# First batch of a spectral-mixing and SwiGLU kernel: tables and filter loaded whole, weights rounded through the first chunk, filter parts on partition halves

## The chip, the cores and the metric

The kernel runs on one core of one Trainium2 chip. The metric is the device time of one execution in microseconds (us). Every time quoted is the median of several executions with its lowest and highest.

## The reference, cut to what matters

```python
X = np.fft.rfft(x, axis=1)                 # x: (8, 3008, 256) float32
y = np.fft.irfft(X * (filt_r + 1j * filt_i)[None], n=3008, axis=1)
y = y.astype(np.float32).reshape(24064, 256)
g = y @ w_gate                              # 256 x 1536, float64
out = ((g / (1 + np.exp(-g))) * (y @ w_val)) @ w_out   # 1536 x 256, float64
```

The three weight matrices arrive as float64 and are brought to fp32 on the chip.

## The kernel before

The Fourier transforms are matmuls in three stages. Stage 1 (`pa`) is a 47-point transform of x, written to DRAM as d1. Stage 2 reads d1 back as `t2`, transforms it over 64 points (`pb`), multiplies it with the filter on VectorE (`p`, `q`), adds on GpSimd, transforms back (`pc`), and writes d2. Stage 3 (`pd`) reads d2 and gives y. The feed-forward follows in blocks of 14 products (`wA_g` and the like; a seven-product scheme for 2x2 blocks of matrices); after every three blocks comes a projection (`wA_o`, `wE_o`, ...), 64 projections in all. The kernel places the tiles that its matmuls write in PSUM; copying one out of it is called its eviction (0.59 us for `g` from a pc of 128x512, on ScalarE). Between the stages results wait in tiles: `t1` (stage 1, on the way to d1), `g` (pc, on the way to d2) and `y`; `s` and `h` hold the two branches of the feed-forward, whose gating product VectorE makes, and `w` and `pw` are the working tiles of a rounding. While batch b goes through the feed-forward, pieces of batch b+1's transforms are filled in between the products. Only batch 0 has nothing to hide under: its transforms, and the rounding of the weights, are the start of the run.

Stage 2, its loads, and one rounding (18 such parts in all):

```python
def load_two(self, u):                       # tables, t2 and filter of one step
    self.tb[u] = tbpool.tile([128, NV, 2, 128], FP32, tag="tb")           # 2 buffers
    nc.sync.dma_start(out=self.tb[u], in_=de_dram[:, ss])
    self.t2[u] = t2pool.tile([128, NV, C], FP32, tag="t2")                # 3 buffers
    self.f[u] = fpool.tile([128, NV, 2, C], FP32, tag="f")
    for p in range(2):
        half = slice(64 * p, 64 * p + 64)
        nc.sync.dma_start(out=self.t2[u][half], in_=self.d1[...])
        nc.sync.dma_start(out=self.f[u][half], in_=f_dram[:, ss])

def stage2a(self, u):
    ps = fps.tile([128, NV, C], FP32, name=f"pb_{self.b}_{u}", tag="f")   # PSUM, 2 buffers
    # ... two matmuls into ps ...
    nc.vector.tensor_tensor(out=pt, in0=ps, in1=f[:, :, 0, :], op=ALU.mult)
    nc.vector.scalar_tensor_tensor(out=qt[lo], in0=ps[hi], scalar=-1.0, in1=f[hi, :, 1, :], ...)
    nc.vector.tensor_tensor(out=qt[hi], in0=ps[lo], in1=f[lo, :, 1, :], op=ALU.mult)
    add(nc.gpsimd, pt, pt, qt)

def stage2b(self, u):
    ps = fps.tile([128, NV, C], FP32, name=f"pc_{self.b}_{u}", tag="f")   # the same two buffers
    # ... two matmuls into ps ...
    nc.scalar.copy(out=g, in_=ps)
    # ... two stores of g to d2, issued by GpSimd ...

def round_weights(j):
    # ... nine VectorE operations on 128 x 512 elements: exponent, sign, mantissa, product ...
    # then three ScalarE copies and four GpSimd adds into wg_t, wv_t or wo_t
```

The order of the start, with cuts:

```python
for k, filt in enumerate((filt_r, filt_i)):  # rearranged copy of the filter in DRAM
    ...nc.scalar.dma_start(out=f_dram[...], in_=...)
for u in range(N_ONE):                       # 16 steps
    spec.stage1(u)
for u in range(N_TWO + 1):                   # 12 steps
    spec.stage2a(u); spec.stage2b(u - 1)
    round_weights(todo.pop(0))
# ... stage 3 of the first chunk ...
while todo:
    round_weights(todo.pop(0))
```

Of the kernel before, what the change touches and what calls it, by code (L numbers as in the profile page):

```python
# [44 lines left out]
NJ = NM // 2  # L45
# [56 lines left out]
def kernel(  # L102
# [22 lines left out]
    t1pool = pool("t1", 2)  # L125
    t2pool = pool("t2", 3)
    fpool = pool("fp", 2)
# [16 lines left out]

    f_dram = fdpool.tile([NQ, NS, 2, C], FP32, name="filt")

# [8 lines left out]
    def weight_parts():  # L155

        cols = [w.bitcast(U32).rearrange("(a p) (h j f two) -> j p h a f two",
                                         a=2, p=128, h=2, j=NJ, two=2)
                for w in (moe_w_gate, moe_w_val)]
        rows = moe_w_out.bitcast(U32).rearrange("(l j p) (c f two) -> j p l c f two",  # L160
                                                l=2, j=NJ, p=128, c=2, two=2)
        for j in range(NJ):
            for w, dst in zip(cols, (wg_t, wv_t)):
                yield w[j], dst[:, j], True
            yield rows[j], wo_t[:, j], False

# [3 lines left out]
    def load_weights(j):  # L170
        if j < len(weights):
            raws[j] = rpool.tile([128, 2, 2, 128, 2], U32, name=f"raw_{j}", tag="raw")
            for i in range(2):
                nc.sync.dma_start(out=raws[j][:, i], in_=weights[j][0][:, i])

    def round_weights(j):



        load_weights(j + 1)  # L180
        raw, (_, dst, left) = raws.pop(j), weights[j]
# [3 lines left out]
        man = w.bitcast(U32)  # L185
        v = nc.vector
        v.tensor_scalar(out=pw, in0=high, scalar1=20, scalar2=0x7FF,
                        op0=ALU.logical_shift_right, op1=ALU.bitwise_and)
        v.tensor_scalar(out=pw, in0=pw, scalar1=-896.0, scalar2=0.0, op0=ALU.add, op1=ALU.max)
        v.tensor_scalar(out=pw, in0=pw, scalar1=255.0, scalar2=None, op0=ALU.min)  # L190
        v.tensor_scalar(out=pw, in0=pw, scalar1=23, scalar2=None, op0=ALU.logical_shift_left)
        flat = "p a b f -> p (a b f)"
        flat2 = "p a b f two -> p (a b f) two"
        v.scalar_tensor_tensor(out=pw.rearrange(flat), in0=raw.rearrange(flat2)[:, :, 1],
                               scalar=0x80000000, in1=pw.rearrange(flat),
                               op0=ALU.bitwise_and, op1=ALU.bitwise_or)
        v.tensor_scalar(out=man, in0=high, scalar1=0xFFFFF, scalar2=None, op0=ALU.bitwise_and)
        v.tensor_scalar(out=w, in0=man, scalar1=2.0 ** -20, scalar2=1.0,
                        op0=ALU.mult, op1=ALU.add)
        v.scalar_tensor_tensor(out=w.rearrange(flat), in0=raw.rearrange(flat2)[:, :, 0],  # L200
                               scalar=2.0 ** -52, in1=w.rearrange(flat),
                               op0=ALU.mult, op1=ALU.add)
        v.tensor_tensor(out=w, in0=w, in1=pw.bitcast(FP32), op=ALU.mult)
        e = nc.gpsimd
# [17 lines left out]
    class Spectral:  # L222
# [10 lines left out]
        def load_x(self, u):  # L233
            if u < N_ONE:
                self.x[u] = xpool.tile([NR, NV, C], FP32, name=f"x_{self.b}_{u}", tag="x")
                rows = x[self.b].rearrange("(r n) c -> r n c", n=32)

                for r in (slice(0, 80), slice(80, NR)):
                    nc.sync.dma_start(out=self.x[u][r], in_=rows[r, ts(u, NV), :])

        def load_two(self, u):
            if u < N_TWO:
                b = self.b
                ss = ts(u, NV)
                self.tb[u] = tbpool.tile([128, NV, 2, 128], FP32, name=f"tb_{b}_{u}", tag="tb")
                nc.sync.dma_start(out=self.tb[u], in_=de_dram[:, ss])
                self.t2[u] = t2pool.tile([128, NV, C], FP32, name=f"t2_{b}_{u}", tag="t2")
                self.f[u] = fpool.tile([128, NV, 2, C], FP32, name=f"f_{b}_{u}", tag="f")
                for p in range(2):
                    half = slice(64 * p, 64 * p + 64)  # L250
                    a0 = p * NS + NV * u
                    nc.sync.dma_start(out=self.t2[u][half],
                                      in_=self.d1[a0:a0 + NV].rearrange("s n c -> n s c"))
                    nc.sync.dma_start(out=self.f[u][half], in_=f_dram[:, ss])

# [4 lines left out]
        def stage1(self, u):  # L260

            if u == 0:
                self.load_x(0)
                self.load_x(1)
            self.load_x(u + 2)
            t1 = t1pool.tile([NK, NV, C], FP32, name=f"t1_{self.b}_{u}", tag="t1")
            ps = fps.tile([128, NV, C], FP32, name=f"pa_{self.b}_{u}", tag="f")
            nc.tensor.matmul(out=ps[0:NK], lhsT=wf_t, rhs=self.x.pop(u), start=True, stop=True)  # L268
            nc.scalar.copy(out=t1, in_=ps[0:NK])
            nc.gpsimd.dma_start(out=self.d1_rows[:, ts(u, NV), :], in_=t1)  # L270

        def stage2a(self, u):
# [6 lines left out]
            for i in range(NV):  # L279
# [4 lines left out]
            lo, hi = slice(0, 64), slice(64, 128)  # L284
            nc.vector.tensor_tensor(out=pt, in0=ps, in1=f[:, :, 0, :], op=ALU.mult)
            nc.vector.scalar_tensor_tensor(out=qt[lo], in0=ps[hi], scalar=-1.0,
                                           in1=f[hi, :, 1, :], op0=ALU.mult, op1=ALU.mult)
            nc.vector.tensor_tensor(out=qt[hi], in0=ps[lo], in1=f[lo, :, 1, :], op=ALU.mult)
            add(nc.gpsimd, pt, pt, qt)
# [167 lines left out]


    nc.sync.dma_start(out=wf_t, in_=wf_dram.ap())
    for k, filt in enumerate((filt_r, filt_i)):  # L460
        for half in range(2):
            off, step = (0, 1) if half == 0 else (N1, -1)
            nc.scalar.dma_start(
                out=f_dram[32 * half:32 * half + 32, :, k, :],
                in_=bass.AP(tensor=filt.tensor, offset=filt.offset + off * C,
                            ap=[[N1 * C, 32], [step * C, NS], [1, C]]))
    nc.scalar.dma_start(out=wi_t, in_=wi_dram.ap())
    spec = Spectral(0)
    with tc.tile_pool(name="raw", bufs=2) as rpool:
        for u in range(N_ONE):  # L470
            spec.stage1(u)
        load_weights(0)
        todo = list(range(len(weights)))
        for u in range(N_TWO + 1):
            if u < N_TWO:
                spec.stage2a(u)
            if u:
                spec.stage2b(u - 1)
            round_weights(todo.pop(0))
        for i in range(2):  # L480
            spec.load_t4(0, i)
        for step in range(4):
            spec.stage3(0, step)
        while todo:
            round_weights(todo.pop(0))

    spool = pool("sp", 2)
    hpool = pool("hp", JB + 1)
    upool = pool("up", 2)
    opool = pool("op", 2)  # L490

# [4 lines left out]
    for b in range(B):  # L496
# [26 lines left out]
        for i in range(NP):  # L523
# [5 lines left out]
            def fill(fills=fills):  # L529
                for piece in fills.pop(0):  # L530
                    piece()

            hidden(b, k, j, cur.y[k], fill)
            if late is not None:
# [35 lines left out]
```

## Time and profile before

The kernel before took 3158.5 us (3158.22 to 3161.21, 3 runs). The table gives landmarks of its profiled execution, read from the timeline of TensorE. A stage's length is the difference of two columns. (The fifth is counted from the second product, `wE_o`, of the second projection to that of the last.)

| first pb | last pc starts | first feed-forward product | first projection | second to 64th projection | span |
|---|---|---|---|---|---|
| 65.42 | 148.09 | 167.98 | 224.57 | 2858.63 | 3156.1 |

The fifth column is the body: there TensorE is busy all the time (2893.15 of 2900 us from 220 to 3120 us), so a microsecond gained before the first projection should be a microsecond off the end. The columns before it are the start, where TensorE waits. The prediction shows the profile's own lines.

### The profile page before, as it was taken

To read this page: it belongs to the slowest core of one execution; us is meant where nothing else is said; L and a number is where in the kernel's file an instruction comes from. 1 tells how busy PE (TensorE), PEld (TensorE's weight loads), DVE (VectorE), ACT (ScalarE), POOL (GpSimd) and SP (SyncE) were. 2 spreads that over 40 slices of the span, in tenths; PEclk is the share of its full clock that TensorE was granted. 3 is DMA by queue.
4 is the path that set the end of the run, shared out by engine and by line. 5 is a ranking of instruction groups with operands and counts; after the bars stand their busy time and mean duration, and the time that the engine had idled before them with its cause. 6 is when DMAs were issued, how large, how long until landed. Compare 5 with 4: busy or idle time off the path is not lost.

```text
span 3156.1 us, 40788 instructions
## 1 busy us (share of the span) xinstructions
PE 3047.2 (97%) x15488; PEld 2243.0 (71%) x15488; DVE 1432.8 (45%) x2306; ACT 1144.6 (36%) x2104; POOL 1387.8 (44%) x1644
## 2 busy tenths in 40 slices
PE   4499999999999999999999999999999999999998
PEld 1266777777776777777777677777777677777776
DVE  4654454345444445335443345434544444544443
ACT  1144334333334333333334433333333433333332
POOL 3444454345443445344444445434544345533343
PEclk9689999999999999999999999999999999999999
DMA  7732332224222233123322233222331223210000
GB/s 224 206 96 70 97 81 73 60 60 111 81 59 70 72 89 96 55 63 88 87 73 60 70 91 87 66 67 60 104 87 55 71 66 93 71 30 20 21 9 12
DMA packets 118291, 240.78 MB, mean 76 GB/s; under 512 B 21712, under 2 KB 55504, under 8 KB 118096
## 3 DMA queue, kind: packets, MB, share of 16 engines
q1 hardware_dynamic: 88224, 160.00, 18.3%
q0 software_dynamic: 26624, 75.01, 8.2%
q10 hardware_dynamic: 3248, 3.18, 0.3%
q8 instruction: 122, 2.00, 0.3%
q14 instruction: 73, 0.60, 0.1%
HBM read 163.13 MB, written 78.12 MB: 76 GB/s over the span
## 4 chain that ended last, share of the span: by engine, by line
PE 83%; POOL 7%; DVE 3%; issue 3%; ACT 1%; DMA 1%; SPq 0%; POOLq 0%; DVEq 0%; ACTq 0%
PE wA_g L357 15%; PE wA_v L357 15%; PE wA_o L421 8%; PE wE_g L357 7%; PE wE_v L357 7%; PE wE_o L421 7%; PE wF_o L421 4%; PE wF_g L357 4%; PE wF_v L357 4%; PE pd L315 4%; POOL o L148 3%; PE pa L268 3%; POOL h L151 3%; PE pb L280 3%; PE pc L297 3%
## 5 line engine op out<-in xcount | busy, mean ns | idle before, releaser
L357 PE MATMUL wA_g<-y,wg_t 128*128 128x376 f32 x1536 | 612.6, 480 | 1.0 <-ACT s L377 1.0
L357 PE MATMUL wA_v<-y,wv_t 128*128 128x376 f32 x1536 | 611.0, 479 | 0.0
L151 POOL TENSOR_TENSOR h<-h 128x376 f32<-128x376 f32 x576 | 564.9, 981 | 28.8
L148 POOL TENSOR_TENSOR h<-h 128x376 f32<-128x376 f32 x192 | 187.7, 978 | 732.1 <-PE wE_v L357 388.7
L366 ACT COPY u_g<-wA_g 128x376 f32<-128x376 f32 x576 | 269.5, 468 | 627.3 <-PE wA_g L357 627.3
L357 PEld LDWEIGHTS wA_v<-y,wv_t 128*128 128x128 f32 x1536 | 291.7, 190 | 194.4 <-DVE h L379 11.7
L421 PEld LDWEIGHTS wA_o<-wo_t,h 128*128 128x128 f32 x3456 | 406.3, 192 | 16.3
L421 PE MATMUL wA_o<-wo_t,h 128*128 128x128 f32 x3456 | 417.5, 275 | 0.0
L357 PEld LDWEIGHTS wA_g<-y,wg_t 128*128 128x128 f32 x1536 | 283.0, 190 | 176.7 <-issue 27.4
L148 DVE TENSOR_TENSOR s<-u_g,wF_g 128x376 f32<-128x376 f32 x192 | 104.9, 546 | 516.0 <-PE wF_g L357 492.4
L384 ACT ACTIVATE s<-s 128x1128 f32<-128x1128 f32 x192 | 219.5, 1143 | 320.8 <-DVE s L148 320.8
L386 DVE TENSOR_TENSOR h<-s,h 128x1128 f32<-128x1128 f32 x192 | 256.0, 1333 | 125.3 <-ACT s L384 125.2
L357 PE MATMUL wE_g<-y,wg_t 128*128 128x376 f32 x768 | 306.0, 480 | 0.0
L357 PE MATMUL wE_v<-y,wv_t 128*128 128x376 f32 x768 | 305.9, 480 | 0.0
L366 ACT COPY u_v<-wA_v 128x376 f32<-128x376 f32 x576 | 272.3, 473 | 72.0 <-PE wA_v L357 68.3
L421 PE MATMUL wE_o<-wo_t,h 128*128 128x128 f32 x2304 | 281.6, 276 | 7.5 <-DVE o L148 7.5
L421 PE MATMUL wF_o<-wo_t,h 128*128 128x128 f32 x2304 | 278.4, 275 | 0.0
L421 PEld LDWEIGHTS wE_o<-wo_t,h 128*128 128x128 f32 x2304 | 267.5, 192 | 13.6 <-DVE o L148 13.6
L421 PEld LDWEIGHTS wF_o<-wo_t,h 128*128 128x128 f32 x2304 | 267.7, 192 | 0.0
L148 DVE TENSOR_TENSOR s<-u_g,wE_g 128x376 f32<-128x376 f32 x384 | 209.1, 544 | 103.8 <-ACT u_g L366 99.8
L148 DVE TENSOR_TENSOR h<-u_v,wE_v 128x376 f32<-128x376 f32 x384 | 209.2, 545 | 28.4 <-ACT u_v L366 5.6
L357 PEld LDWEIGHTS wE_g<-y,wg_t 128*128 128x128 f32 x768 | 146.5, 191 | 97.4 <-issue 0.9
(67 smaller groups left out, 3180.4 us busy)
## 6 DMA issues: line engine op xcount, KB each, us to landing
f<-filt SPq DMA_DIRECT2D x192, 256.0 KB
tb<-de_tbl SPq DMA_DIRECT2D x96, 256.0 KB
d<-t POOLq DMA_DIRECT2D x128, 192.0 KB, 2.4
t<-d SPq DMA_DIRECT2D x192, 128.0 KB
d<-g POOLq DMA_DIRECT2D x192, 128.0 KB, 2.7
t<-d SPq DMA_DIRECT2D x64, 384.0 KB
x<-in_x_dram SPq DMA_DIRECT2D x128, 160.0 KB
out_dram<-o POOLq DMA_DIRECT2D x128, 128.0 KB, 2.0
```

Of the source, the lines that this page charges most:

```text
L148: eng.tensor_tensor(out=dst, in0=a, in1=b, op=ALU.add)
L151: eng.tensor_tensor(out=dst, in0=a, in1=b, op=ALU.subtract)
L268: nc.tensor.matmul(out=ps[0:NK], lhsT=wf_t, rhs=self.x.pop(u), start=True, stop=True)
L280: nc.tensor.matmul(out=ps[:, i, :], lhsT=self.tb[u][:, i, 0, :], rhs=t2[:, i, :], start=True, stop=True)
L297: nc.tensor.matmul(out=ps[:, i, :], lhsT=tb[:, i, 1, :], rhs=pt[:, i, :], start=True, stop=True)
L315: nc.tensor.matmul(out=psv[:, n, :], lhsT=self.t4[k, i][:, n, ts(cb, 128)], rhs=wi_t, start=True, stop=True)
L357: nc.tensor.matmul(out=bk[z][kind], lhsT=wt[z][:, j, LEFT[p], :], rhs=y[:, RIGHT[p], :], start=start, stop=True, skip_group_check=True)
L366: nc.scalar.copy(out=u[(1, 6, 7).index(p)], in_=bk[z]["A"])
L384: nc.scalar.activation(out=s[:, 0:3], in_=s[:, 0:3], func=AF.Silu)
L386: nc.vector.tensor_tensor(out=h[:, 0:3], in0=s[:, 0:3], in1=h[:, 0:3], op=ALU.mult)
L421: nc.tensor.matmul(out=bk[kind][:, t, :], lhsT=hs[i][:, HID[p], t0:t0 + 128], rhs=wo_t[:, JB * q + i, RIGHT[p], :], start=start and t == 0 ...
```

## The change

Its intent: give batch 0 the memory that the feed-forward uses only later, and load the stage-2 tables and the whole filter into it at once, so that no load is left in the stage-2 loop; load x in four pieces; take VectorE's work for the weights from nine operations to six and spread the second half of it over the first chunk's blocks. The filter's real and imaginary parts lie on partitions 0 to 63 and 64 to 127, which halves its loads and its tile, at the price of four half-size products in place of three. The diff, cut:

```diff
-    t2pool = pool("t2", 3)
+    t2pool = pool("t2", 2)
-    f_dram = fdpool.tile([NQ, NS, 2, C], FP32, name="filt")
+    f_dram = fdpool.tile([128, NS, C], FP32, name="filt")
     # ... rounding: order of the parts; load_weights(j + 2) ...
+        v.tensor_scalar(out=man, in0=high, scalar1=0xFFFFF, scalar2=None, op0=ALU.bitwise_and)
+        nc.scalar.activation(out=w, in_=man, func=AF.Copy, scale=2.0 ** -20, bias=1.0)
         v.tensor_scalar(out=pw, in0=high, ...)
         v.tensor_scalar(out=pw, in0=pw, scalar1=-896.0, scalar2=0.0, op0=ALU.add, op1=ALU.max)
-        v.tensor_scalar(out=pw, in0=pw, scalar1=255.0, scalar2=None, op0=ALU.min)
-        v.tensor_scalar(out=pw, in0=pw, scalar1=23, scalar2=None, op0=ALU.logical_shift_left)
+        v.tensor_scalar(out=pw, in0=pw, scalar1=255.0, scalar2=2.0 ** 23, op0=ALU.min, op1=ALU.mult)
-        v.tensor_tensor(out=w, in0=w, in1=pw.bitcast(FP32), op=ALU.mult)
+        nc.gpsimd.tensor_tensor(out=w, in0=w, in1=pw.bitcast(FP32), op=ALU.mult)
     # ... load_x: for batch 0, four loads of 8 positions ...
+        def load_tables(self, parts=3):
+            tb = spool0.tile([128, NS, 2, 128], FP32, name="tb0")
+            f = spool0.tile([128, NS, C], FP32, name="f0")
+            for i in range(parts):
+                nc.sync.dma_start(out=tb[:, ts(i, n)], in_=de_dram[:, ts(i, n)])
+                for rows, view in filter_parts():        # four pieces of 32 partitions
+                    nc.sync.dma_start(out=f[rows, ts(i, n), :], in_=view(n * i, n))
     # ... stage1: four t1 buffers for batch 0 ...
-            nc.vector.tensor_tensor(out=pt, in0=ps, in1=f[:, :, 0, :], op=ALU.mult)
+            for h in (lo, hi):
+                nc.vector.tensor_tensor(out=pt[h], in0=ps[h], in1=fr, op=ALU.mult)
     # ... start: with a pool "start" that ends before the feed-forward's pools begin ...
+        spec.load_x(0); load_weights(0); load_weights(1); spec.load_tables()
-    opool = pool("op", 2)
+    opool = pool("op", 1)
     # ... first chunk:
+            if b == 0 and i == 0:
+                for rows, view in filter_parts():
+                    nc.scalar.dma_start(out=f_dram[rows], in_=view(0, NS))
+            for _ in range((2, 3, 2, 2, 2, 3)[i] if todo else 0):
+                round_weights(todo.pop(0))
```

## The prediction

> **What bounds the kernel now.** I read the busy slices of the page first. Over the body TensorE is busy in nine tenths of every slice; only the first two slices (79 us each) stand at four.
>
> ```profile
> PE   4499999999999999999999999999999999999998
> DVE  4654454345444445335443345434544444544443
> PEclk9689999999999999999999999999999999999999
> ```
>
> So I split the run into windows. From 220 to 3120 us TensorE is busy 2893 of 2900 us: nothing is to be won there, and what the change does to the other engines there (VectorE 45%) costs nothing unless it becomes a wait. The start is another matter. Columns: stretch, length, then busy us (instructions) of PE, weight loads, DVE, ACT, POOL, granted clock, DMA share, GB/s.
>
> ```profile
> 20.00:40.00 20.00, 11.32 (x13) 2.85 (x13) 10.77 (x22) 5.60 (x19) 9.75 (x19) 1.00 0.73 220
> 80.00:100.00 20.00, 10.84 (x24) 7.34 (x24) 6.20 (x9) 1.68 (x4) 7.22 (x9) 0.74 0.69 197
> 140.00:160.00 20.00, 5.83 (x12) 3.67 (x12) 18.02 (x33) 3.26 (x11) 10.59 (x18) 0.50 0.75 218
> 180.00:200.00 20.00, 15.38 (x38) 8.36 (x37) 12.96 (x23) 9.12 (x18) 7.58 (x15) 0.66 0.40 123
> 200.00:220.00 20.00, 20.00 (x64) 11.71 (x64) 10.03 (x16) 9.44 (x18) 9.53 (x11) 1.00 0.00 0
> ```
>
> TensorE is busy 206.75 us of the first 300, so about 93 us of idle is all that can be gained, and part of the busy time is at a low clock. In that start four stretches follow each other, read from the timeline: stage 1 of batch 0 (to 54 us), stage 2 (65.4 to 150.2), the round trip of stage 3 through DRAM (150.2 to 168.0, the first feed-forward product), and a disturbed first feed-forward block (168 to about 200).
>
> Stage 1 and stage 2 wait for buffers. From the lists of waits up to 205 us, the sync queue's own and then ScalarE's (total us, times, longest):
>
> ```profile
> SPq L246 <- PE pc L297: 39.3, 11, 7.1
> SPq L239 <- PE pa L268: 26.2, 16, 6.2
> ...
> ACT t L269 <- DMA d<-t: 30.9, 15, 6.7
> ```
>
> L246 is the load of a table pair, which may go only when the second transform (pc) two steps back has freed one of two buffers. One step of stage 2 on the timeline:
>
> ```profile
> 88.90 2.04 PE L280 MATMUL pb<-t,tb 128*128 128x256 f32 x4 [3.43 <-issue]
> 90.98 0.69 DVE L285 TENSOR_TENSOR p<-pb,f 128x512 f32<-128x512 f32 x1 [5.08 <-DMA t<-d]
> 91.68 0.69 DVE L286 SCALAR_TENSOR_TENSOR q<-pb,f 64x512 f32<-64x512 f32 x1
> 92.39 0.68 DVE L288 TENSOR_TENSOR q<-pb,f 64x512 f32<-64x512 f32 x1
> 92.58 0.33 SPq L246 DMA_DIRECT2D tb<-de_tbl  x1
> 94.13 1.27 POOL L148 TENSOR_TENSOR p<-p,q 128x512 f32<-128x512 f32 x1
> 95.80 2.04 PE L280 MATMUL pb<-t,tb 128*128 128x256 f32 x4 [3.25 <-DMA tb<-de_tbl]
> ```
>
> The reader is to see 6.9 us from pb to pb: 3.7 from pb's start until the table load is issued, 3.2 until the table is there. VectorE's products were over at 93.1, so without that load pb could have gone 2.7 us earlier.
>
> The disturbed block: VectorE still had some four weight roundings queued ahead of the first evictions.
>
> ```profile
> 187.00 0.69 DVE L203 TENSOR_TENSOR w<-w,pw 128x512 f32<-128x512 f32 x1
> 190.03 0.55 DVE L148 TENSOR_TENSOR s<-u_g,wF_g 128x376 f32<-128x376 f32 x1 [2.34 <-POOL wo_t L151]
> ```
>
> Between 168.0 and 200.3 TensorE did 19 feed-forward products, 7 pa and two steps of pd: 19 x 0.63 + 7 x 0.86 + 2 x 0.45 = 18.9 us at full clock (durations from 330 to 347 us and the chain), so 13.4 us were lost.
>
> [...] from 10 to 22 us ScalarE's queue took 53.1% and the sync queue 48.9% of the engines' time. [...] The trace has 689 ns on 128 and 684 on 64 partitions, so a half costs as much as a whole. [...] the masking of a weight took 0.42 us alone, 1.49 beside a GpSimd add. [...] Here pb takes 2.04 us at a stretch's mean clock of 0.74, and some 0.86 in the body.
>
> **The change part by part**, with the order of instructions as the changed program builds it.
>
> (1) Stage 1. x comes in four loads instead of sixteen, with four t1 buffers instead of two: the 26 us and 31 us of waits above mostly go. But the sync queue now holds tables and filter ahead of t2. Until the first t2 load: x 3.1, tables 3.1, filter 3.1, four weight parts 1.0 MB; besides them d1 3.1 MB written, and the DRAM copy of the filter, 3.1 MB, which the scheduler puts first on ScalarE's queue although the source issues it in the first feed-forward block. Sum 16.6 MB (before: 15.8 MB in 70 us). The best stretch, 10 to 22 us, moved 344 GB/s, the mean was 225. At 320 that is 52 us; with 3 us for t2, pb starts at 55 instead of 65.4. Gain 10, uncertain by 6.
>
> (2) Stage 2. The table load leaves the loop; p is now two products on halves, four at 0.69 = 2.8 us. The loop that is left goes through the one PSUM buffer that pb reuses: 2.0 (pb) + 2.8 + 0.2 for hand-overs = 5.0 us. Where TensorE gets the full clock pb takes 1 us and the loop 4. I take 4.7 on average. Some 14 rounding operations of about 0.55 us lie in between, mostly under pb. First two steps 2.1 + 5.6, ten more 47, last add and pc 3.4: 58 us, plus 2 for stalls: 60 instead of 84.8. Gain 25, uncertain by 7.
>
> (3) Stage 3 stays: 17.8 us from the last pc to the first product. So the feed-forward begins at 55 + 60 + 18 = 133 instead of 168: 35 us.
>
> (4) Rounding. Nine operations on VectorE become six; the linear step goes to ScalarE (0.58 us), the last product to GpSimd (about 1.3). By the means of the groups before (0.75, 0.42, 0.47, 0.56, 0.72, 0.74) six cost 3.7 us. But in the built order only nine of 18 are done before y; the others sit among the evictions of blocks 0 to 3, with single buffers for w and pw. VectorE there: 8.7 roundings x 3.7 = 32, plus four blocks' evictions at 6 x 0.545 + 0.55 + 1.33 = 5.15 each, 20.6, together 52.6 us; plus about 1 us per rounding for GpSimd's product and four adds before w may be overwritten: 61. TensorE needs 4 x 14 x 0.63 + 8 x 0.86 + 0.9 = 43. VectorE becomes the bound of these blocks: 18 us lost instead of 13.4. Cost 5, range -3 to +12.
>
> (5) Body. The extra half product is 84 x 0.69 = 58 us of VectorE over the whole run, off the path. The filter loads halve (512 to 256 KB a step), which nothing waited for. One output buffer instead of two: three blocks, some 30 us, lie between a chunk's last store and the next write; stores take 2 us. Zero.
>
> Sum: -35 + 5 = -30, so 3128 us.
>
> **The rivals.** (a) The loads at the start are bound by bandwidth: the same bytes must pass before t2, the filter copy still competes, pb starts no earlier. For it: DMA share 0.73 to 0.84 in the first 40 us. Against: the waits for buffers in the same stretch. It makes 3138. (b) The roundings in the first chunk cost as much as the start gains, since GpSimd has per block two roundings at 3.4 plus 4 us of h [...]: 35 us lost there, 3145 to 3150. Against: the block before was also held up by roundings. (c) Stage 2 runs with the clock up and loads overlap fully: pb at 48, 4.1 us a step, start at 119: 3112. (d) Some wait enters the body: a single microsecond per chunk is 32 us. Against: all new buffer distances are a whole block or more.
>
> **Range and chances.** Terms of 6, 7 and 7 us, taken as independent, give about 12; a tail upward for (b) and (d). Two per cent is 63 us: more than two thirds of all idle at the start, so faster than that is very unlikely; slower would need (d) in the body.
>
> **What will show it.** Right: the wait of L246's successor for pc gone from stage 2, pb to pb 4 to 5 us, the first feed-forward product near 133 us, VectorE busy above 80% from there for 60 us, windows after that unchanged. Wrong: first pb at 65 or later (rival a), the product start early but block 4 no earlier than before (b), TensorE below 99% in the body (d).

Cut from the prediction, where marked, are rules of the hardware that no trace of this case shows. What the traces measured: in the paragraph before the parts these are the shares of two queues in the time of the DMA engines; VectorE's products of 512 elements on 128 and on 64 partitions; the masking of a weight (0.42 us at 112.60 with no GpSimd operation beside it, 1.49 at 129.71 beside a GpSimd add of 1.43); and pb, which lasts 2.04 us at 88.90 and 1.03 in the body. The 0.86 there is the distance to the next start (340.63 to 341.49). The sum comes to -35 + 5 = -30, from 3158 to 3128 us.

## The result, and the profile after

The changed kernel took 3156.48 us (3155.42 to 3162.7, 4 runs); the kernel before, in the same rounds, 3158.36 us (3157.76 to 3161.21, 4 runs). The ratio is 0.9996, with a 95% interval of 0.9979 to 1.0014. The two kernels are equally fast, and 3156.48 lies 28 us above the predicted 3128, more than twice the 12 us that the prediction gives its terms together.

The profiled execution of the changed kernel was the slowest of its four (a span of 3160.8 us). The busy slices of its page:

```profile
PE   4689999999999999999999999999999999999998
...
DVE  2664554345544445335543355434554345544443
PEclk9589999999999999999999999999999999999999
```

TensorE's second slice has gone from 4 to 6, and its third from 9 to 8: work has moved ahead, and something behind it has been lost. Windows of 20 us over the start say where. Columns as in the prediction: stretch, length, busy us (instructions) of PE, weight loads, DVE, ACT, POOL, granted clock, DMA share, GB/s.

```profile
20.00:40.00 20.00, 13.04 (x15) 3.08 (x13) 3.49 (x6) 5.41 (x13) 10.63 (x18) 1.00 1.06 307
40.00:60.00 20.00, 7.11 (x8) 2.04 (x8) 0.00 (x0) 3.49 (x6) 3.08 (x6) 1.00 1.05 261
...
100.00:120.00 20.00, 16.05 (x32) 8.90 (x30) 12.90 (x21) 2.89 (x8) 12.43 (x17) 0.50 0.49 131
...
160.00:180.00 20.00, 15.62 (x41) 8.02 (x40) 14.60 (x23) 10.35 (x23) 12.94 (x18) 0.91 0.33 105
180.00:200.00 20.00, 14.54 (x37) 7.12 (x35) 17.31 (x24) 7.34 (x18) 14.62 (x19) 0.91 0.33 102
200.00:220.00 20.00, 14.73 (x48) 8.56 (x48) 13.26 (x21) 9.36 (x23) 14.65 (x20) 0.88 0.28 91
```

Three things are to be seen. From 20 to 60 us the DMA engines are busy all the time (1.06 and 1.05; 0.73 before in 20 to 40). From 100 to 120 us, in stage 2, TensorE is busy 16 of 20 us at half its clock. From 160 to 220 us the feed-forward runs with TensorE busy some 15 of 20 us; before, the last of these windows was full. The landmarks beside those of before, and of a second run of the unchanged new kernel (the run called control below):

| | first pb | last pc starts | first product | first projection | body | span |
|---|---|---|---|---|---|---|
| before | 65.42 | 148.09 | 167.98 | 224.57 | 2858.63 | 3156.1 |
| after | 66.00 | 133.48 | 153.92 | 224.39 | 2863.14 | 3160.8 |
| after again | 62.59 | 129.29 | 149.71 | 219.92 | 2862.89 | 3156.1 |

Feed-forward begins 14 to 18 us earlier, but the blocks up to the first projection take 70 us and not 57, so the first projection is only 0 to 5 us earlier; and the body is 4 us longer. Nothing is left.

**Stage 1 and the loads.** From TensorE's timeline after:

```profile
48.17 7.11 PE L305 MATMUL pa<-x,wf_t 94*96 94x512 f32 x8 [9.75 <-DMA x<-in_x_dram]
66.00 3.75 PE L317 MATMUL pb<-t,tb 128*128 128x256 f32 x8 [10.72 <-DMA t<-d]
```

The waits for buffers that the prediction found are mostly gone (up to 66 us ScalarE waits 12.6 us for stores of t1 in place of 25.9, and the loads of x 3.3 us for pa in place of 15.7), and TensorE waits for transfers in their place: 9.75 us for the last quarter of x, and 10.72 us for t2, which stands behind tables, filter and weights. 18.34 MB had passed by 66 us, a mean of 278 GB/s.

**Stage 2.** One step on the timeline after, to be set beside the step from 88.90 us in the prediction:

```profile
91.13 2.08 PE L336 MATMUL pc<-p,tb 128*128 128x256 f32 x4
...
93.24 0.59 ACT L339 COPY g<-pc 128x512 f32<-128x512 f32 x1 [3.82 <-PE pc L336]
93.88 2.07 PE L317 MATMUL pb<-t,tb 128*128 128x256 f32 x4 [0.68 <-ACT g L339]
...
94.13 1.18 POOL L342 DMA_DIRECT2D d<-g  x2 [2.50 <-ACT g L339]
95.32 1.28 POOL L160 TENSOR_TENSOR p<-p,q 128x512 f32<-128x512 f32 x1
...
96.65 2.07 PE L336 MATMUL pc<-p,tb 128*128 128x256 f32 x4 [0.70 <-POOL p L160]
```

The table load is gone from the step. What closes the loop now is not VectorE. From pc to pc: 2.1 us of pc, 0.6 of ScalarE's eviction, then GpSimd, which has waited 2.50 us for that eviction, issues the stores of g (1.18) and only then adds p and q (1.28), on which the next pc waits: 5.5 us. pb runs beside GpSimd, but it may start only when ScalarE has evicted pc, because both use the same two PSUM buffers (psum, below, tests this). From the third pb to the last it is 5.27 us a step, (125.61 - 78.22) / 9. The list of waits between 66 and 136 us (total us, times, longest) carries both hand-overs; a wait for a table is no longer in it:

```profile
PE pc L336 <- POOL p L160: 13.9, 8, 5.7
...
PE pb L317 <- ACT g L339: 7.0, 10, 0.7
```

**The first blocks.** TensorE's timeline again, first product and first projection:

```profile
153.92 1.51 PE L396 MATMUL wA_g<-y,wg_t 128*128 128x376 f32 x2
...
224.39 2.59 PE L460 MATMUL wA_o<-wo_t,h 128*128 128x128 f32 x18
```

That is 70.5 us for what the prediction counted as 43 us of TensorE's work. VectorE's groups of instructions from 150 to 225 us (line, engine, operation, shapes, count; busy us, mean ns of one; idle just before them, and what ended most of it):

```profile
L211 DVE TENSOR_SCALAR pw<-pw 128x512 uint32<-128x512 uint32 x9 | 6.7, 749 | 0.2
...
L425 DVE TENSOR_TENSOR h<-s,h 128x1128 f32<-128x1128 f32 x3 | 6.2, 2077 | 0.4 <-ACT s L423 0.3
...
L206 DVE TENSOR_SCALAR w<-raw 128x512 uint32<-128x512 uint32 x9 | 6.1, 680 | 11.9 <-POOL wo_t L163 6.7 <-POOL wg_t L163 3.5 <-POOL wv_t L163 1.7
L208 DVE TENSOR_SCALAR pw<-raw 128x512 uint32<-128x512 uint32 x9 | 4.3, 483 | 5.5 <-POOL w L219 5.5
```

Nine roundings lie here. Their six operations have means of 944, 749, 736, 684, 680 and 483 ns, 4.28 us together and 38.5 us for nine. To that comes idle time of 11.9 + 5.5 = 17.4 us in which VectorE waits for GpSimd: L206 overwrites w, and GpSimd's last add must have read it; L208 overwrites pw, and GpSimd's product must have read it. The wait is passed on: from 150 to 225 us ScalarE's step L207 waits 14.1 us for L206 (nine times), with evictions behind it in ScalarE's order, and TensorE 9.2 us for evictions of u_v (five times). The gating product L425 takes 2077 ns on average; the prediction had 1330. All three of these start within 0.01 us of GpSimd's product L219, which the change has moved there, and in each pair one of the two is slow: twice L425 takes 2.45 us beside 1.27 (the first is shown), and at 206.59 L425 keeps its 1.33 us and L219 takes 2.45:

```profile
172.10 1.27 POOL L219 TENSOR_TENSOR w<-w,pw 128x512 f32<-128x512 f32 x1 [4.58 <-ACT s L423]
172.11 2.45 DVE L425 TENSOR_TENSOR h<-s,h 128x1128 f32<-128x1128 f32 x1 [0.15 <-ACT s L423]
```

**The body.** From 300 to 3100 us TensorE is busy 2793.4 of 2800 us before and 2792.5 after, and yet the body takes over 4 us longer. One chunk's stage 3 on TensorE, before:

```profile
404.65 1.92 PE L315 MATMUL pd<-wi_t,t 96*128 96x94 f32 x16
```

And the same piece of work after:

```profile
401.84 0.36 PE L354 MATMUL pd<-wi_t,t 96*128 96x94 f32 x2
...
404.31 0.36 PE L354 MATMUL pd<-wi_t,t 96*128 96x94 f32 x2
...
405.80 1.47 PE L354 MATMUL pd<-wi_t,t 96*128 96x94 f32 x12
```

The sixteen matmuls stand together before and are cut in three after, with feed-forward products between them: the built order differs. From each pd line to the start of the next product the timeline has 1.75 us before, and 0.47 + 0.20 + 1.31 = 1.98 us after; two products that follow a cut take 0.74 and 0.66 us to the next in place of 0.63. That makes 0.23 + 0.11 + 0.03 = 0.37 us. Per batch of eight projections, one interval is 0.40 us longer and three are 0.08 us longer, 0.64 us; seven batches that have a next batch under them make 4.5 us.

### The profile page after: what moved, and what is told of

Read it like the earlier page. It is cut to its first block, busy times and chain, and to the rows that moved or that the text cites. A ratio compares the mean times of both kernels' runs of the same rounds, so it can differ in the third digit from the quotient of the medians. Undisturbed runs are those within 1.5% of the kernel's fastest.

```text
span 3160.8 us, 40740 instructions
## 1 busy us (share of the span) xinstructions
PE 3059.3 (97%) x15488; PEld 2241.2 (71%) x15488; DVE 1474.2 (47%) x2348; ACT 1150.4 (36%) x2122; POOL 1418.7 (45%) x1662
## 4 chain that ended last, share of the span: by engine, by line
PE 78%; POOL 7%; DVE 5%; issue 2%; ACT 2%; POOLq 0%; DVEq 0%
PE wA_v L396 15%; PE wA_g L396 15%; PE wA_o L460 7%; PE wE_v L396 7%; PE wE_g L396 7%; PE wE_o L460 7%; PE wF_o L460 4%; PE wF_g L396 4%; PE pd L354 3%; PE wF_v L396 3%; POOL o L160 3%; PE pa L305 3%; POOL h L163 3%; PE pc L336 2%; PE pb L317 2%
## 5 line engine op out<-in xcount | busy, mean ns | idle before, releaser
L460 PEld LDWEIGHTS wA_o<-wo_t,h 128*128 128x128 f32 x3456 | 406.9, 192 | 16.6 <-issue 0.6
L425 DVE TENSOR_TENSOR h<-s,h 128x1128 f32<-128x1128 f32 x192 | 258.2, 1345 | 125.6 <-ACT s L423 125.5
L160 POOL TENSOR_TENSOR p<-p,q 128x512 f32<-128x512 f32 x96 | 121.9, 1270 | 212.0 <-DVE q L327 207.3
```

What stands on the lines that cost most here:

```text
L160: eng.tensor_tensor(out=dst, in0=a, in1=b, op=ALU.add)
L425: nc.vector.tensor_tensor(out=h[:, 0:3], in0=s[:, 0:3], in1=h[:, 0:3], op=ALU.mult)
L460: nc.tensor.matmul(out=bk[kind][:, t, :], lhsT=hs[i][:, HID[p], t0:t0 + 128], rhs=wo_t[:, JB * q + i, RIGHT[p], :], start=start and t == 0 ...
```

## The experiments

My theories, and against each its rival: the loads hold up the first pb (by the filter's copy in DRAM, or by the order and bulk of tables and filter ahead of t2); the shared PSUM buffers set the stage-2 loop (or VectorE does); the roundings take the start's gain back in the blocks (by VectorE's own time, or by the single buffers between VectorE and GpSimd); and the body is longer for the built order that the filter's halves bring (or for fewer t2 and output buffers). Times of runs from different rounds are compared through their ratios to the kernel before, whose median was 3161.23, 3159.26, 3159.97 and 3159.56 us in the four sets. All these ratios lie within 2% of 1; a gain in time is read only where the interval keeps clear of the control's. The rest is read from landmarks, which come from one profiled execution of each kernel and, between sets, from different chips.

### control: the changed kernel again

No edit.

> The changed kernel itself, as a control for the runs above and for the spread of its start: its profiled run (3160.8 us) was the slowest of four, and three kernels with the same stage 1 had pb at 61.9, 62.3 and 71.2 us where that run had it at 66.0. If the start varies from run to run with the DMA, this profile should show another first pb (61 to 71 us) and shift first product and first projection by the same amount, the body between the second and the last projection again 2863.1 us (before: 2858.6). Time 3155 to 3158; the kernel before 3158 to 3161.

Measured: 3157.95 us (3155.52 to 3161.89, 5 runs), ratio 0.9995 (0.9983 to 1.0008). The result repeats. Between two profiled executions of the same code the first pb moved from 66.00 to 62.59 us and everything after it with it, so differences of up to about 4 us in the first column mean nothing by themselves. One thing differs: this profile records a granted clock of 1.00 from 80 to 140 us (0.997 over the whole run, against 0.985), where the first recorded 0.63 and 0.50, and yet pb takes 2.07 us in both, twice the 1.03 of the body. The recorded clock of a window is thus not to be trusted alone; the durations tell more.

### nocopy: no rearranged copy of the filter in DRAM

```diff
-                    nc.sync.dma_start(out=self.f[u], in_=f_dram[:, ss])
+                    for rows, view in filter_parts():
+                        nc.sync.dma_start(out=self.f[u][rows], in_=view(NV * u, NV))
-                for rows, view in filter_parts():
-                    nc.scalar.dma_start(out=f_dram[rows], in_=view(0, NS))
```

> The changed kernel without the DRAM copy of the filter: batches 1 to 7 load each step's filter straight from the inputs in four pieces. Theory A (the start is bound by DMA bytes; 18.3 MB moved by 66 us in the changed kernel, 3.15 of them this copy, at 278 GB/s): first pb at about 55 us instead of 66, first feed-forward product at 143 instead of 153.9, the first projection at 214 instead of 224.4, time 3146, 10 us under the changed kernel. Theory B (the nine roundings that are left form a chain of their own and set when block 3 ends, whatever the start of the feed-forward): pb and the first product earlier, but the projection still at 221 to 225 and the time within 3 us of the changed kernel. Body unchanged in both.

Measured: correct, 3155.06 us (3153.17 to 3157.91, 5 runs), ratio 0.9981 (0.9968 to 0.9995). TensorE's timeline:

```profile
60.32 3.75 PE L316 MATMUL pb<-t,tb 128*128 128x256 f32 x8 [24.54 <-DMA t<-d]
```

Stage 1 was done at 36 us (the changed kernel's at 55, the control's at 52), and then TensorE stood still for 24.54 us until t2 came: the first pb is only 2.3 us ahead of the control's, which is within the spread, and the ratio's interval overlaps with the control's. The bulk freed was used by stage 1, but t2 still stands behind all of the tables and the filter. The theory that the copy alone costs some 10 us falls; a place in the queue behind the tables is what is left of it.

### psum: batch 0's pb in PSUM banks of its own

The feed-forward's banks are idle during stage 2.

```diff
-            ps = fps.tile([128, NV, C], FP32, name=f"pb_{self.b}_{u}", tag="f")
+            if self.b == 0:
+                ps = wps.tile([128, 512], FP32, name=f"pb_{self.b}_{u}", tag="A").rearrange(
+                    "p (a c) -> p a c", a=NV)
+            else:
+                ps = fps.tile([128, NV, C], FP32, name=f"pb_{self.b}_{u}", tag="f")
```

> The changed kernel with pb of batch 0 in the PSUM banks that the feed-forward does not use yet, so that pb no longer waits for ScalarE's eviction of pc (0.7 us idle and the order pb-pc-eviction in each step). First pb at 66 as before. Theory A: the step falls from 5.3 to about 4.2 us (VectorE's four products 2.8 plus a share of rounding, or 4.15 of TensorE at half clock), stage 2 ends at 122 to 125 instead of 135.6, first product at 142; fewer roundings fit before it, so blocks 0 to 3 lose more; projection at 216 to 220, time 4 to 8 us under the changed kernel. Theory B: first product at 142, projection at 224 again, time the same within 3 us.

Measured: correct, 3151.79 us (3151.3 to 3153.29, 5 runs), ratio 0.9972 (0.9959 to 0.9984). From the first pb (61.88) to the start of the last pc (112.55) it is 50.7 us; the control has 66.7. A window of this run:

```profile
80.00:100.00 20.00, 13.24 (x46) 8.82 (x44) 16.23 (x23) 3.79 (x9) 15.92 (x21) 0.91 0.72 214
```

The granted clock is 0.91 and VectorE and GpSimd are the busy ones, where the changed kernel had 0.63 in the same window and 0.50 in the next. The durations agree: pb takes 1.10 us from 94 to 105 us here and 2.07 in the control. So the shared buffers set the loop: 16 us, the clock's part included. Why the clock rises with them apart is not shown: TensorE is less busy here than in the changed kernel (13.24 of 20 us against 16.05 in the window from 100 us), and its gaps between 94 and 109 us reach 2.9 us. Of these only 6 or 7 arrive at the end (the ratio's interval just touches the control's). The first projection is 16.3 us earlier than the control's (203.60), but it is 57.05 us to the second, in place of 47.55: the roundings had not caught up.

### wdbl: two buffers for the rounded weight

```diff
-        w = rpool.tile([128, 2, 2, 128], FP32, name=f"w_{j}", tag="w")
+        w = rpool.tile([128, 2, 2, 128], FP32, name=f"w_{j}", tag="w", bufs=2)
-            t1 = p1.tile([NK, NV, C], FP32, name=f"t1_{self.b}_{u}", tag="t1", bufs=2)
+            t1 = p1.tile([NK, NV, C], FP32, name=f"t1_{self.b}_{u}", tag="t1",
+                         bufs=2 if p1 is t1pool else 1)
```

The second edit pays for the memory: three t1 buffers instead of four in stage 1.

> The changed kernel with two buffers for the rounded part w (and one t1 buffer less in stage 1 of batch 0, for the room). In the changed kernel VectorE waited 11.9 us for w and 5.5 us for pw between 150 and 225 us. If those waits are the loss: the 11.9 go, projection at 213 to 216 and time 8 to 10 us under the changed kernel. If VectorE and GpSimd are short of time rather than of buffers (58 us and 52 us busy of these 75, each slowed by the other), 2 to 4 us.

(That each is slowed by the other: 2.45 us in place of 1.33 for L425 and of 1.27 for L219 in The first blocks.)

Measured: correct, 3154.3 us (3153.78 to 3156.26, 5 runs), ratio 0.998 (0.9967 to 0.9992). From the first product to the first projection it is 63.0 us (155.41 to 218.45) against the control's 70.2, and VectorE's wait for w in that stretch is 0.3 us against 8.2. But the first pb came at 71.18, 8.6 us after the control's, so most of that did not reach the end: the first projection is 1.5 us earlier, and the ratio's interval overlaps with the control's. Because the first product is later, one rounding fewer falls behind it (7 against 8), so the 7 us are not the buffer's alone. I put the late pb down to noise then; the last run shows that it was the t1 buffer.

### noround: no rounding in the first chunk

Parts 9 to 17 use the upper words of the raw weights as they are; the result is wrong.

```diff
+        if j >= 9:
+            w = raw.bitcast(FP32)[:, :, :, :, 1]
+        else:
             # ... the rounding ...
```

> Wrong on purpose: from the tenth weight part on, the high words are used as they are, without the six VectorE operations, ScalarE's step and GpSimd's product; copies, adds and loads stay. Measures what rounding in the first chunk costs. First product at 152 to 154. If the roundings are the whole loss of blocks 0 to 3 (70.5 us from first product to projection against 43 of TensorE's work), the projection starts at 198 to 203 and the time is 22 to 26 us under the changed kernel. If GpSimd's h and weight adds or late weight loads hold the blocks as well, 210 and 12 us.

Measured: 3137.38 us (3136.11 to 3139.83, 4 runs), ratio 0.9926 (0.9912 to 0.9939). The start up to the first product is the control's (149.52), and the first projection comes at 200.55, 19.4 us earlier. A window of it:

```profile
160.00:180.00 20.00, 16.78 (x46) 8.37 (x45) 6.61 (x12) 11.20 (x28) 13.55 (x26) 0.92 0.54 181
```

VectorE's busy time has fallen from 14.60 to 6.61 us. The nine roundings of the first chunk cost 19 us, and the body leaves that untouched.

### halves: the kernel before with only the filter's halves

```diff
-    f_dram = fdpool.tile([NQ, NS, 2, C], FP32, name="filt")
+    f_dram = fdpool.tile([128, NS, C], FP32, name="filt")
-            nc.vector.tensor_tensor(out=pt, in0=ps, in1=f[:, :, 0, :], op=ALU.mult)
+            for h in (lo, hi):
+                nc.vector.tensor_tensor(out=pt[h], in0=ps[h], in1=fr, op=ALU.mult)
     # ... and one load of 256 KB a step in place of two of 256 KB ...
```

> The kernel before with one part of the change alone: filter parts on partition halves (four products of 64 partitions per step instead of three, half the filter bytes). The changed kernel's body is 4.5 us longer, 0.64 us in each of seven batches, all in the four chunks' intervals in which stage 2 is filled in. If the fourth product of VectorE does it: 2863 us between second and last projection here too, and 0.4 us in the fifth interval of each batch. If it is the third t2 buffer or the second output buffer that the change takes away: 2858.6 as before. The start should gain a little, since each step of stage 2 loads 256 KB less: first projection 220 to 226. Time within 5 us of before either way.

Measured: correct, 3155.13 us (3154.03 to 3156.99, 4 runs), ratio 0.9986 (0.9973 to 1.0). The body is 2862.87 us, 4.2 longer than before: the halves alone bring the whole of it, with three t2 and two output buffers as before, which clears those. The first projection is 5 us earlier (219.48), so this part about pays for itself; its ratio's interval reaches 1. Its pd is cut in the same three pieces.

### bits: the rounding as three bit operations

A float64 in fp32's normal range becomes the truncated fp32 by moving bits: sign and top exponent bit from the upper word, the next 27 bits shifted by three, and three bits from the lower word. It truncates where the old way rounds. No step on ScalarE or GpSimd is left but the copies and the four adds.

```diff
-        # six VectorE operations, one of ScalarE, one of GpSimd; buffers w and pw
+        w = rpool.tile([128, 2, 2, 128], FP32, name=f"w_{j}", tag="w", bufs=2)
+        v.tensor_scalar(out=bits, in0=hi, scalar1=3, scalar2=0x3FFFFFF8,
+                        op0=ALU.logical_shift_left, op1=ALU.bitwise_and)
+        v.scalar_tensor_tensor(out=bits, in0=hi, scalar=0xC0000000, in1=bits,
+                               op0=ALU.bitwise_and, op1=ALU.bitwise_or)
+        v.scalar_tensor_tensor(out=bits, in0=lo, scalar=29, in1=bits,
+                               op0=ALU.logical_shift_right, op1=ALU.bitwise_or)
```

> The changed kernel with a shorter rounding: three bitwise operations of VectorE per weight part (exponent and mantissa shifted together, sign, three low bits; truncated, exact to one unit in the last place) instead of six, ScalarE's step and GpSimd's product, and two buffers for w. By the durations of the trace 0.4 + 0.7 + 0.7 = 1.8 us of VectorE instead of 4.3, and 1.4 us of GpSimd less per part. If the roundings are what the first four blocks lost (27 us over TensorE's work): they shrink to at most 5, first projection at 197 to 203 when first pb is at 62, time 3133 to 3140, as in the run without rounding (3137.4). Rival: copies and adds of the parts (ScalarE 0.9, GpSimd 2 us each) hold the blocks: projection at 210.

Measured: correct, 3129.2 us (3126.61 to 3134.11, 4 runs), ratio 0.9905 (0.989 to 0.992). From the first product to the first projection it is 48.6 us (144.15 to 192.71) against the control's 70.2, and stage 2 ends 2.5 us earlier too.

### bits_psum: both

> The short rounding and pb of batch 0 in the idle PSUM banks together. psum alone moved the first product from 150 to 133 (first pb at 62) but lost 9.5 us in the second projection's interval, 57.1 instead of 47.6 us, where roundings were late. With the short rounding that loss should go: first product 130 to 133, first projection 177 to 183, second interval 47.6 to 49, time 3115 to 3122. If GpSimd (adds of weight parts, p, stores) has become the limit of stage 2, the step stays at 4.2 us and the projection comes at 188 to 192, time 3127.

The edit is that of bits and that of psum together. Measured: correct, 3119.41 us (3117.68 to 3121.61, 4 runs), ratio 0.9873 (0.986 to 0.9887). The first projection is at 184.05, and it is 47.56 us to the second: with light roundings, what psum gains is no longer given back there. It is 9.8 us faster than bits alone, where psum alone was 6 to 7 faster than the changed kernel.

### late_only: two thirds of tables and filter held back until the first t2

nocopy, and tables and filter as three tiles. The first third is loaded ahead. The second and third get a one-element GpSimd add that reads the first and the third step's t2, so that their loads come after these in the queue.

```diff
+            if after is not None:
+                for first in (tb[0:1, 0, 0, 0:1], f[0:1, 0, 0:1]):
+                    add(nc.gpsimd, first, after[0:1, 0, 0:1], after[0:1, 0, 0:1])
+            nc.sync.dma_start(out=tb, in_=de_dram[:, ts(i, n)])
```

> The changed kernel without the DRAM copy of the filter, and with only the first third of tables and filter loaded ahead; the second and third parts are held back by a small GpSimd add that reads t2 of steps 0 and 2, so that their loads stand behind the first t2 loads in the sync queue. In the run without the copy alone TensorE had finished stage 1 at 36 us and waited 24.5 us for t2, which stood behind 6.3 MB of tables and filter. If that queue is what kept the first pb at 62: pb at 38 to 44, first product at 125 to 133, first projection at 196 to 204, body 2863 us, time 3130 to 3138. If the loads are short of bandwidth wherever they stand, stage 2 then waits for the later parts and the first product comes at 140 or later, time above 3144.

Measured: correct, 3148.85 us (3147.89 to 3149.04, 5 runs), ratio 0.9964 (0.9952 to 0.9977). The first pb stands at 46.15, 16.4 us ahead of the control's. Stage 2 takes 6 us more (46.15 to 119.30 against 62.59 to 129.29), and the first product is 10 us earlier. So the bulk ahead of t2 did hold up the start.

### late: bits, psum and the loads of late_only

> The same loads together with the short rounding and pb of batch 0 in the idle PSUM banks. The three gains lie in different stretches: against the run of the last two together (first pb 63.3, first product 130.0, projection 184.1, 3119.4 us) the whole should move by what pb moves, some 20 us: first pb 38 to 44, first product 106 to 114, projection 160 to 170, time 3096 to 3103. If fewer roundings then fit before the first feed-forward block, part of it comes back there: projection 172, time 3107. Body 2863 us.

Measured: correct, 3116.98 us (3114.91 to 3118.12), ratio 0.9862 (0.9847 to 0.9877), the lowest median, though its interval overlaps with that of bits_psum. From its timeline:

```profile
46.90 3.78 PE L317 MATMUL pb<-t,tb 128*128 128x256 f32 x8 [10.55 <-DMA t<-d]
```

The first pb is 16.4 us earlier than in bits_psum, but the last pc (108.82) only 3.3 us: stage 2, which takes 48.8 us there, takes 61.9 here. Tables and filter now pass during it, but that this is the reason is not shown: after the first pb TensorE waits only 3.3 us for t2, and 23.8 us for GpSimd's adds of p and q (13.2 in bits_psum); up to 83 us the built order has pb and pc in pairs, and each pc takes 2.07 or 2.08 us, twice the 1.03 of the body.

### late_full: late, and the filter of batches 1 to 7 as before

Full filter tile and three products for batches 1 to 7; memory paid with one w buffer and two t1 buffers.

> The last kernel, with batches 1 to 7 back at three products per step on a filter tile that holds both parts on both halves (eight pieces per load; to fit, one w buffer and two t1 buffers less). In its built program TensorE's order over the last 6000 rows is the one of the kernel before, where the changed kernel differs in 103 places (pd matmuls placed one by one between feed-forward products). If that order is the body's 4.5 us: body 2858.6 us, time 4 us under the last kernel, 3092 to 3100. If the loads in eight pieces cost more than that, body 2863 or more. Stage 1 with two t1 buffers may lose 2 to 5 us at the start.

Measured: correct, 3127.75 us (3126.84 to 3129.89), ratio 0.99 (0.9886 to 0.9913). The body is 2858.90 us, that of before, and its pd stands in one piece again. The start is 13.8 us longer (first projection 194.46 against late's 180.62).

### both_fixes: late with before's products in the body and a start almost its own

As late_full, but paid with one g buffer in batches 1 to 7, and one t1 buffer in batch 0 (three, not four).

```diff
-    gpool = pool("gp", 2)
+    gpool = pool("gp", 1)
-            t1 = p1.tile([NK, NV, C], FP32, name=f"t1_{self.b}_{u}", tag="t1", bufs=2)
+            t1 = p1.tile([NK, NV, C], FP32, name=f"t1_{self.b}_{u}", tag="t1",
+                         bufs=2 if p1 is t1pool else 1)
     # ... filter tile and products of batches 1 to 7 as before ...
```

> The run called late with its start left almost as it was (two buffers for the rounded weights; three buffers for t1 instead of four), and in batches 1 to 7 the filter tile and the three products of the kernel before, paid for with one g buffer instead of two there. If the start's gain and the body's 4.5 us are independent, as I hold, the body is 2858.9 from the second to the last projection (late 2862.9), the first projection stands at 180 to 185 us, and the time is 3111 to 3117, against 3117 for late. Rival 1: the single g buffer becomes a wait in the body and it is 2863 or more: 3117 or slower. Rival 2: what late_full lost at the start (14 us) came from the larger filter tile's traffic and not from the single buffer for the rounded weights: first projection near 194 again, 3126 to 3129.

Measured: correct, 3123.66 us (3121.41 to 3126.02, 4 runs), ratio 0.9884 (0.9867 to 0.99). The body is 2859.00 us, so the single g buffer costs nothing there and Rival 1 falls. But the first projection stands at 192.37, 7 to 12 us later than I expected and near the 194 of Rival 2. The rival's reason does not hold: the loss arises in the first 57 us, with the first pb at 56.44, 9.5 us after late's, and the sync queue issues no load of the larger filter tile before that. The waits of TensorE in the first 60 us name the cause. In both_fixes:

```profile
PE pa L302 <- ACT t L303: 10.6, 8, 4.0
```

In late:

```profile
PE pa L298 <- ACT t L299: 0.2, 1, 0.2
```

With three t1 buffers pa waits 10.6 us for ScalarE to free its PSUM buffer, and ScalarE in turn for stores of t1 (12.2 us in three waits); with four, pa waits 0.2 us, and ScalarE 7.3. So the fourth t1 buffer is worth about 10 us. This also fits late_full, whose two t1 buffers put its first pb at 55.81, 8.9 us after late's, of which 7.3 are left at its first product; the other 6.5 us of its loss lie between its first product and first projection (134.15 to 194.46, 60.3 us, against late's 53.8), where it has one w buffer: VectorE waits 19.8 us there for GpSimd to have read w, in both_fixes with two buffers 3.1 us in 54.6. I did not find room for all of it in one kernel.

All runs by landmarks (us; the body is from the second to the last projection):

| run | first pb | last pc starts | first product | first projection | body | median |
|---|---|---|---|---|---|---|
| control | 62.59 | 129.29 | 149.71 | 219.92 | 2862.89 | 3157.95 |
| nocopy | 60.32 | 127.33 | 147.75 | 218.26 | 2862.97 | 3155.06 |
| psum | 61.88 | 112.55 | 132.94 | 203.60 | 2862.93 | 3151.79 |
| wdbl | 71.18 | 135.32 | 155.41 | 218.45 | 2862.95 | 3154.3 |
| noround | 62.30 | 129.11 | 149.52 | 200.55 | 2862.96 | 3137.38 |
| halves | 66.94 | 148.03 | 166.40 | 219.48 | 2862.87 | 3155.13 |
| bits | 63.98 | 126.78 | 144.15 | 192.71 | 2862.86 | 3129.2 |
| bits_psum | 63.34 | 112.09 | 129.97 | 184.05 | 2862.89 | 3119.41 |
| late_only | 46.15 | 119.30 | 139.66 | 209.33 | 2862.91 | 3148.85 |
| late | 46.90 | 108.82 | 126.82 | 180.62 | 2862.85 | 3116.98 |
| late_full | 55.81 | 116.87 | 134.15 | 194.46 | 2858.90 | 3127.75 |
| both_fixes | 56.44 | 119.38 | 137.82 | 192.37 | 2859.00 | 3123.66 |

## Why the prediction was wrong

The prediction's steps imply a first projection at 133 + 61 = 194 us and an unchanged body. The control has 219.92 us and 4.3 us more in the body. Added to 3128 these 26 and 4 us give 3158, which is the control's time. That the time would stay within 2% was right. Step by step, against the control:

| step | predicted | measured | difference |
|---|---|---|---|
| (1) first pb | 55 | 62.6 | +7.6 |
| (2) stage 2 | 60 | 68.8 | +8.8 |
| (3) stage 3 and back | 18 | 18.4 | +0.4 |
| (4) blocks to the first projection | 61 | 70.2 | +9.2 |
| (5) body, change | 0 | +4.3 | +4.3 |

**(1) "At 320 that is 52 us": the rate was mis-sized, and the waiting line left out.** The bytes were nearly right (16.6 MB for 18.34 moved by 66 us), but the mean rate was 278 GB/s with the DMA engines busy throughout, where the step took 320 from a stretch of 12 us. It also counted only bytes and not who stands behind whom: nocopy takes 3.1 MB away and the first pb moves by 2.3 us against the control; late_only takes that and two thirds of tables and filter out of t2's way and it moves by 16.4. The number of rival (a), a first pb at 65, is what the first profile showed; its cause, bytes that must pass before t2, fits late_only, but the copy was not the main part of them. Which packets take the engines' time is not settled: in nocopy the engines were just as busy at 253 GB/s.

**(2) "The loop that is left goes through the one PSUM buffer that pb reuses ... 5.0 us": the wrong chain.** The removed table load was read correctly, and it is gone. But the step assumed that pb waits for VectorE's products. In the trace pb starts just when the pc before it has been evicted (at 93.88, the eviction ending at 93.83): it takes pc's buffer, and waits for ScalarE. And GpSimd queues the stores before its add; 5.27 us a step in place of the 4.7 taken on average, and 12.2 us to the third pb in place of 7.7. Both were to be seen before the change. The step of stage 2 that the prediction shows has these two lines as well, which it leaves out, the second of them just ahead of GpSimd's add at 94.13:

```profile
92.63 0.58 ACT L300 COPY g<-pc 128x512 f32<-128x512 f32 x1 [6.16 <-PE pc L297]
93.52 0.59 POOL L303 DMA_DIRECT2D d<-g  x1 [5.06 <-ACT g L300]
```

The clock added to it: the 4.7 counted on some time at full clock, and from 86 us on every pb and pc took 2.07 or 2.08 us, twice the 1.03 of the body. psum, which changes only the buffers, takes 16 us off the stage; how much of that is the clock's no run separates. What lowers the clock is not shown, and the lengths of TensorE's gaps do not settle it: pb took 1.13 us at 82.95, and after a gap of 2.07 us pc took 2.08; from 89 to 131 us the gaps are at most 0.83 us, and the granted clock stood at 0.50 from 100 to 120 us with TensorE busy 16.05 of 20 us. In psum gaps of up to 2.9 us from 94 to 109 us went with a pb of 1.10 us and a granted clock of 0.91 and 0.78 in the windows from 80 and 100 us.

**(3)** was right.

**(4) "Cost 5": the term for VectorE's roundings and for GpSimd's delays was mis-sized.** The mechanism and its place were right: VectorE's queue in blocks 0 to 3 bounds them. The step took 3.7 us per rounding from the means of before, and "about 1 us per rounding" for GpSimd. Measured are 4.28 us and 17.4 / 9 = 1.93 us. This is 9 x (0.58 + 0.93) = 13.6 us more; the blocks were 9 us longer than predicted, so part of it lay beside other work. (The blocks' start counts too: what is rounded before the first product is not rounded after it, and differs between the runs.) The sign that the step had named, VectorE busy above 80% for 60 us, did not show: the three windows from 160 us have 73, 87 and 66%, since it waited in between. The change moved a product to GpSimd, and the two engines' work was slower side by side: L425 took 2.45 us, in place of 1.33 in the body, beside GpSimd's product of 1.27 us, or kept its 1.33 and the product took 2.45. The prediction had seen such a slowing in the trace of before, 0.42 to 1.49 us, but only for the masking of a weight, and did not count it for L425. Shown by runs: the roundings as a whole 19 us (noround); the shorter rounding with its second w buffer, 21.6 us of the blocks (bits). The single w buffer alone is at most 7 us (wdbl), and what the slowing side by side adds no run separates. Rival (b), that the roundings cost as much as the start gains, is what happened.

**(5) "Zero": the step looked only at waits.** No wait appeared, TensorE is as busy as before, and still the body grew by 4 us. The step asked what the extra product does to VectorE and to buffers, not what it does to the order in which matmuls are built. halves brings the 4 us, late_full and both_fixes take it away, and each time pd is cut or whole accordingly. No run has four products with pd whole, so that the cut and not the products is the cause rests on the 0.37 us counted in the timeline and is not shown by itself. Rival (d) had the right place and the wrong sign to look for: TensorE below 99%.

Where did the expected 30 us go, then? About 17 were never gained (steps 1 to 3), 9 were given back in the blocks, and 4 in the body. (One sum of the prediction is off: rival (c), a start at 119 in place of 133, makes 3114 and not 3112.)

## What to carry to other kernels

When a load leaves a loop, write down the next chain from the built order, buffer by buffer and queue by queue, before taking a number for it: here the next chain was a PSUM buffer shared by two stages and a store queued before an add. Work moved to another engine was no relief here, where the two wait for each other at single buffers (17.4 us of VectorE's idle time) and are slower side by side (2.45 us in place of 1.33); fewer operations on fewer engines (three bit operations and a second buffer in place of eight operations) took 29 us off the changed kernel. Taken together, own PSUM banks, light roundings and loads behind the first data that need them make a kernel of 3116.98 us, 1.4% under the kernel before. Gains do not simply add: against the control, bits and psum give 29 and 6 us alone and 38.5 together, while the held-back loads, with the copy gone, give about 9 alone and only 2 to 4 more on top of the two.
